# A gated-recurrence and feed-forward kernel on TensorE: k's transposes, masks, loads and the order of attention's passes from the ninth chunk on

## The chip, the cores and the metric

The kernel runs on one core of a Trainium2 chip. A core has TensorE (PE, matrix products; its weight loads are listed as PEld), VectorE (DVE), ScalarE (ACT), GpSimd (POOL) and SyncE (SP), which here only issues transfers. The metric is the device time of one execution in microseconds (us); lower is better. The profile's span of the execution is some 2 us shorter than that time.

## The reference

A gated linear recurrence over 768 tokens, for 4 sequences of 8 heads of size 48, and then a feed-forward block with SiLU on the 3072 resulting rows. Cut to what is computed:

```python
# q, k, v, alpha: (4, 8, 768, 48) float32; alpha in 0.8 .. 1.0
state = np.zeros((B, H, D, D))
for t in range(S):
    state = alpha[:, :, t, :, None] * state + np.einsum('bhd,bhe->bhde', k[:, :, t], v[:, :, t])
    y[:, :, t] = np.einsum('bhd,bhde->bhe', q[:, :, t], state)
x = y.transpose(0, 2, 1, 3).reshape(B * S, H * D)       # (3072, 384)
h = x @ w_in                                            # w_in (384, 2048)
out = (h * (1 / (1 + np.exp(-h)))) @ w_out              # w_out (2048, 384)
```

## The kernel before

The kernel cuts the tokens into 24 chunks of 128 (6 of each of the 4 sequences, taken in turn: chunk `n` is part `ci = n // 4` of sequence `b = n % 4`). Inside a chunk the recurrence is a masked attention: k is multiplied by a running product of alpha (`kp`), q by a running quotient (`qp`), `kp` and `qp` give the scores, the scores are masked to earlier tokens, and the masked scores times v are the values. What earlier chunks left in the state `st` is added with another product, and at the end of a chunk the state takes up the chunk's k and v, except in the last chunk of each sequence.

The feed-forward block is cut into pieces of about 2.6 us of TensorE each (`enter`: x times w_in, in a form with fewer products than the plain one; `leave`: g times w_out, likewise). A function `fill` sets pieces between attention's stages, so that TensorE has work while other engines prepare the next stage. The framework then orders the instructions of each engine; an instruction goes freely within its dependences unless `keep_in_program_order` pins it behind the one traced before it on its engine. Each engine takes its own instructions strictly in that order.

From chunk 9 on (`n >= NA`, `NA = 8` counted from 0) q, k and alpha are loaded so that VectorE's transposes alone turn them, and the products are laid out in halves of 64 tokens, of which one quarter of a score block is not needed and never computed.

The stages that the change touches (`...` marks cuts):

```python
    def products(n):                          # alpha, k -> kp ; then q -> qp in quotient()
        ...
        dve.tensor_tensor_scan(u[:, end - 1 :: -1], sg[:, end:0:-1], one[:, end:0:-1], 0.0, ALU.mult, ALU.add)
        dve.tensor_single_scalar(least[:, n, :], u[:, 0:end:W], 2.0**-64, ALU.max)
        kp = c["kp"] = turns(kps, n)          # one buffer from chunk 9 on
        ...
    def quotient(n, sg=None, q=None):
        ...
        p = turns(qps, n)                     # one buffer from chunk 9 on
        dve.tensor_tensor_scan(p[:, 0:end], sg[:, 0:end], iv[:, 0:end], 0.0, ALU.mult, ALU.add)
        ...
    def blank(n):                             # clears two PSUM banks for the scores
        if n < NA:
            return
        ps = ctxs[n]["blank"] = [ps_attn() for _ in range(2)]
        for t in ps:
            act.activation(t.rearrange("p j c -> p (j c)"), ident[:, 0:1].to_broadcast([128, 4 * C]),
                           AF.Copy, scale=0.0)

    def scores(n):
        c = ctxs[n]
        ci, b = c["ci"], c["b"]
        ps = c.pop("blank") if n >= NA else [ps_attn() for _ in range(2)]
        for j in (0, 2, 1, 3):
            for e in range(2 if n >= NA else 1):
                for u in range(2):
                    ...
                    pe.matmul(ps[u][at, j, t], lhsT=c["kp"][r, j, at], rhs=c["qp"][r, j, t],
                              start=True, stop=True)
        g = c["g"] = work.tile([128, 2, NP, C], F32, name="g")
        for u in range(2):
            if n < NA:
                act.copy(g[:, u], ps[u])
                gps.affine_select(g[:, u], g[:, u], ...)
                continue
            m = mask[:, :, None, :]
            dve.tensor_tensor(g[:, u].rearrange("p (o j) c -> p o j c", o=2),
                              ps[u].rearrange("p (o j) c -> p o j c", o=2),
                              m.to_broadcast([128, 2, NP // 2, C]), ALU.mult)
        if ci < NCH - 1:
            ps_k = ps_attn()
            for j in range(NP):               # NP = 4
                pe.transpose(ps_k[:, j, :], c["kp"][:, j, :], ident)
            c["kn"] = work.tile([128, NP, C], F32, name="kn")
            act.copy(c["kn"], ps_k)
        if ci > 0:
            s = st[b].rearrange("p j u e -> p j (u e)")
            for j in range(NP):
                act.mul(s[:, j], s[:, j], least[:, n, j : j + 1])

    def values(n):
        ...
        for i, (at, w, x) in enumerate(todo): # 16 products of v with g, 12 of the state with qp
            t, at = divmod(at, 4)
            pe.matmul(py[32 * at : 32 * at + 32, t, :], lhsT=w, rhs=x, ...)
        ...
        act.copy(xts[half][:, :, e * C : (e + 1) * C], py[:, 0:NKT])

    def states(n):
        ...
        if ci < NCH - 1:
            ps = ps_attn()
            for j in range(NP):
                for i in range(4):
                    r = slice(32 * i, 32 * i + 32)
                    pe.matmul(ps[r, j, 0:D], lhsT=c["kn"][:, j, r], rhs=vn[:, 2 * j + i // 2, 0:D],
                              start=True, stop=True)
            for u in range(2):
                ...
                if ci > 0:
                    dve.tensor_tensor(s, x, s, ALU.add)
```

The loop, and where the pieces of the feed-forward block come in:

```python
    for step in range(STEPS):
        ...
        stages = [[(scores, 1)], [(products, 0)], [(values, 1)], [(states, 1)]]
        ...
        elif step >= NA:
            stages = [[(scores, 1)], [(products, 0)], [(values, 1), (states, 1)], [(quotient, 0), (blank, 0)]]
        for slot, group in enumerate(stages):
            for stage, lag in group:
                n = step - lag
                ...
                stage(n)
                ...
                if stage is quotient and n + 1 < NT:
                    load(n + 1)
            fill(step, slot)
```

The results of `leave` are stored from tiles of 128x192 by SyncE (`nc.sync.dma_start(out[...], o)`), 48 stores in all.

## Time and profile before

Three runs took 561.36, 561.52 and 562.27 us, the median is 561.52. The profiled execution has a span of 559.1 us with 12435 instructions.

| engine | busy, us | share of the span | instructions |
|---|---|---|---|
| PE (matrix products) | 543.4 | 97% | 5074 |
| PEld (weight loads, beside PE) | 492.6 | 88% | 5074 |
| DVE (VectorE) | 448.1 | 80% | 821 |
| ACT (ScalarE) | 208.9 | 37% | 414 |
| POOL (GpSimd) | 20.8 | 4% | 44 |

The costliest groups on PE are those of the feed-forward block: 768 and 576 records of 128x192 for `leave` (133.6 and 100.0 us busy), 384 of 128x256 for the plain first pieces (88.3 us) and 640 of 128x256 for `enter` (161.4 us in four groups). Attention's groups are smaller: values 44.7 us, scores 38.2 us, states 12.3 us, transposes of k for the state 13.1 us. A float32 product shows as two records in the trace.

How to read it: a row of a group gives busy time and mean length of one instruction. Products overlap, so busy time divided by the count is less than the mean length. The chain of work that ended last is followed back from the last instruction, at each step to what released it. A line such as L982 is a line of the kernel: L759 the scores, L776 k's transposes, L802 the values, L817 the states, L860 the plain first pieces, L884 `enter`, L982 `leave`.

### The profile page before, as it was taken

How to read it: one execution, taken by the hardware profiler on the slowest of the kernel's cores; microseconds unless marked ns; L12 is line 12 of the kernel's file. 1: busy time of each engine (PE TensorE's matmuls, PEld its weight loads, DVE VectorE, ACT ScalarE, POOL GpSimd, SP SyncE). 2: the span in 40 equal slices, each digit the busy share in tenths (PEclk: the TensorE clock that was granted, in tenths of full speed). 3: DMA queues.
4: the chain of work that ended last, by engine and by line, in shares of the span. 5: the costliest groups of instructions: out<-in, count | busy, mean ns of one | idle time of the engine just before them, and what ended most of it. 6: DMA issues, size and time to landing. Idle time of an engine off the chain costs nothing.

```text
span 559.1 us, 12435 instructions
## 1 busy us (share of the span) xinstructions
PE 543.4 (97%) x5074; PEld 492.6 (88%) x5074; DVE 448.1 (80%) x821; ACT 208.9 (37%) x414; POOL 20.8 (4%) x44
## 2 busy tenths in 40 slices
PE   5999999999999999999999999999999999999996
PEld 3788887898999999899989999999898999999995
DVE  5887789956998799986998897899895885857731
ACT  3456653323233342442433442443443342332100
POOL 5110000300000000000000000000000000000000
PEclk9899999999999999999999999999999999999999
DMA  9999871143443333333425444435422123334200
GB/s 208 223 288 201 235 187 42 26 118 100 101 107 97 82 86 88 98 87 86 130 69 162 141 113 133 131 81 154 132 69 88 53 84 118 101 98 122 72 30 26
DMA packets 94417, 63.81 MB, mean 114 GB/s; under 512 B 55312, under 2 KB 86032, under 8 KB 94352
## 3 DMA queue, kind: packets, MB, share of 16 engines
q1 hardware_dynamic: 94352, 62.94, 43.2%
q8 instruction: 41, 0.67, 0.5%
q14 instruction: 24, 0.20, 0.1%
HBM read 58.20 MB, written 4.72 MB: 113 GB/s over the span
## 4 chain that ended last, share of the span: by engine, by line
PE 79%; DVE 12%; DMA 3%; ACT 2%; SPq 1%; issue 1%; POOL 0%; DVEq 0%; ACTq 0%
PE ps_o L982 35%; PE ps_m L884 21%; PE ps_m L860 11%; PE ps_a L802 6%; PE ps_a L759 3%; PE ps_a L776 2%; DMA qn<-in_q_dram 1%; DVE g L898 1%; DMA bits<-in_moe_w_in_dram 1%; DVE u L701 1%; PE ps_a L817 1%; DVE p L730 1%; DVE seen L665 1%; SPq L456 1%; DVE w_out L626 1%
## 5 line engine op out<-in xcount | busy, mean ns | idle before, releaser
L982 PE MATMUL ps_o<-w_out,g 128*128 128x192 f32 x768 | 133.6, 328 | 0.0
L982 PEld LDWEIGHTS ps_o<-w_out,g 128*128 128x128 f32 x768 | 125.5, 190 | 2.7 <-issue 0.6
L982 PE MATMUL ps_o<-wt,g 128*128 128x192 f32 x576 | 100.0, 327 | 0.0
L982 PEld LDWEIGHTS ps_o<-wt,g 128*128 128x128 f32 x576 | 95.1, 190 | 1.5
L860 PE MATMUL ps_m<-xt,w_in 128*128 128x256 f32 x384 | 88.3, 382 | 0.8 <-ACT xt L807 0.8
L860 PEld LDWEIGHTS ps_m<-xt,w_in 128*128 128x128 f32 x384 | 71.1, 190 | 10.6 <-ACT xt L807 1.2
L884 PE MATMUL ps_m<-xc,w_in 128*128 128x256 f32 x288 | 70.1, 379 | 0.0
L884 PEld LDWEIGHTS ps_m<-xc,w_in 128*128 128x128 f32 x288 | 54.0, 190 | 6.4 <-DVE g L898 0.2
L665 DVE TENSOR_REDUCE seen<-bits 128x1 f32<-128x384 int32 (+2 forms) x65 | 42.4, 689 | 15.1 <-DMA bits<-in_moe_w_out_dram 14.9
L895 ACT ACTIVATE g<-g 128x1024 f32<-128x1024 f32 x32 | 33.1, 1055 | 56.5 <-DVE g L898 56.5
L987 DVE TENSOR_TENSOR g<-g 128x512 f32<-128x512 f32 x72 | 48.4, 685 | 6.0 <-PE ps_o L982 5.9
L890 ACT COPY g<-ps_m 128x512 f32<-128x512 f32 x64 | 36.7, 586 | 36.1 <-PE ps_m L884 36.0
L884 PE MATMUL ps_m<-xc,wx 128*128 128x256 f32 x192 | 50.1, 383 | 0.0
L782 ACT ACTIVATE st<-st,least 128x96 f32<-128x96 f32 x80 | 24.1, 364 | 57.3 <-DVE least L704 57.3
L884 PEld LDWEIGHTS ps_m<-xc,wx 128*128 128x128 f32 x192 | 35.0, 190 | 4.2 <-issue 0.4
L898 DVE TENSOR_TENSOR g<-ps_m,g 128x512 f32<-128x512 f32 x56 | 37.3, 681 | 0.7 <-PE ps_m L884 0.5
L701 DVE TENSOR_TENSOR_SCAN u<-al,one 128x516 f32<-128x516 f32 x24 | 29.1, 1211 | 8.7 <-POOL mask L535 4.5
L730 DVE TENSOR_TENSOR_SCAN p<-al,inv 128x516 f32<-128x516 f32 x24 | 29.4, 1225 | 5.2 <-PE ps_a L802 4.9
L863 ACT ACTIVATE g<-ps_m 128x512 f32<-128x512 f32 x32 | 19.0, 594 | 38.7 <-PE ps_m L860 38.6
L802 PE MATMUL ps_a<-g,vn 128*32 128x128 f32 x768 | 27.9, 281 | 1.8 <-POOL g L766 1.7
L802 PEld LDWEIGHTS ps_a<-g,vn 128*32 128x32 f32 x768 | 20.4, 111 | 9.1 <-issue 5.6
L890 ACT COPY part<-ps_m 128x512 f32<-128x512 f32 x32 | 18.6, 582 | 21.8 <-PE ps_m L884 17.6
(125 smaller groups left out, 632.1 us busy)
## 6 DMA issues: line engine op xcount, KB each, us to landing
bits<-in_moe_w_in_dram SPq DMA_DIRECT2D x24, 512.0 KB, 4.8
bits<-in_moe_w_out_dram SPq DMA_DIRECT2D x32, 384.0 KB, 3.3
at<-in_alpha_dram SPq DMA_DIRECT2D x64, 96.0 KB, 2.3
kt<-in_k_dram SPq DMA_DIRECT2D x64, 96.0 KB, 2.4
qt<-in_q_dram SPq DMA_DIRECT2D x64, 96.0 KB, 2.5
bits<-in_alpha_dram SPq DMA_DIRECT2D x9, 512.0 KB, 3.4
out_dram<-o SPq DMA_DIRECT2D x48, 96.0 KB, 1.7
an<-in_alpha_dram SPq DMA_DIRECT2D x8, 192.0 KB, 5.2
```

Source lines behind the costliest of these rows:

```text
L665: dve.tensor_reduce(seen[kind][which][:, i : i + 1], x, axis=AX, op=op, apply_absolute_value=True))
L701: dve.tensor_tensor_scan(u[:, end - 1 :: -1], sg[:, end:0:-1], one[:, end:0:-1], 0.0, ALU.mult, ALU.add)
L730: dve.tensor_tensor_scan(p[:, 0:end], sg[:, 0:end], iv[:, 0:end], 0.0, ALU.mult, ALU.add)
L782: act.mul(s[:, j], s[:, j], least[:, n, j : j + 1])
L802: pe.matmul(py[32 * at : 32 * at + 32, t, :], lhsT=w, rhs=x, start=(i < 4), stop=(i >= len(todo) - 4), skip_group_check=True)
L860: pe.matmul(ps[:, e, :], lhsT=w_in[:, t, (f + e) * 128 : (f + e + 1) * 128], rhs=xt[:, t, :], start=(t == 0), stop=(t == NKT - 1))
L884: pe.matmul(ps[:, e], lhsT=block_w(w)[:, 2 * pair + e], rhs=block_x(grp, x), start=(first and e == 0), stop=(e == 1), skip_group_check=True)
L890: act.copy(to, ps)
L895: act.activation(x, x, AF.Silu)
L898: dve.tensor_tensor(to, a, b, op)
L982: pe.matmul(ps, lhsT=x, rhs=w[:, i], start=(first and i == 0), stop=(i == HF - 1), skip_group_check=True)
L987: dve.tensor_tensor(cells(grp, h, pair, *to), cells(grp, h, pair, *x), cells(grp, h, pair, *y), ALU.subtract)
```

## The change

From chunk 9 on:

- k for the state is no longer transposed by PE. `flip` lets VectorE transpose `kp` in blocks of 32x32 and stores the tile to DRAM; `land`, one step later, loads it back with four transfers that put the blocks in place. Its PSUM bank and ScalarE's copy go too.
- Masks: no clearing of PSUM before the scores and no product with a mask on VectorE. ScalarE copies the computed parts of the scores to SBUF (two copies of 128x256 elements, four of 64x128), and GpSimd masks the diagonal blocks in place with four selects of 64x256. The part that is never computed is zeroed once.
- Order: attention's products are pinned in program order (`in_order`), also ScalarE's scaling of the state and the sums for `enter`. The stages of a step are set anew: state and values last in the step, with `flip` behind them. The pieces come one slot later (`+ 3` for `+ 2`) and are left to the scheduler.
- Loads of alpha, k and q for the next chunk are issued one by one, each right behind the transpose that frees its tile, not all together at the end. The scaled q has a second buffer.
- 40 of the 48 output stores are issued by GpSimd instead of SyncE, and the output tile has three buffers for two.

The diff, cut to its core (`...` marks cuts; context left out):

```diff
+    def in_order(ins):
+        return tc.keep_in_program_order(ins) if late else ins
...
-    opool = pool("opool", 2)
+    opool = pool("opool", 3)
+    dram = pool("dram", 2, bass.MemoryType.DRAM)
...
-    mask = consts.tile([128, 2, C], F32, name="mask")
-    ...
+    decayed = fix.tile([128, 2 * NP * C], F32, name="g")
+    low, high = slice(0, CH), slice(CH, C)
+    earlier, later = [(low, 0), (high, 1)], [(low, 1), (high, 0)]
...
                 if name == "a":
                     turned(c[name], tokens(sg))
+                    load(n + 1, "a")
...
             turned(c["k"], ps["k"])
+            load(n + 1, "k")
...
-        p = turns(qps, n)
+        p = turns(qps if n < NA else [qps[0], late["p"]], n)
...
             turned(c["q"], q)
+            load(n + 1, "q")
...
-    def blank(n):
-        ...
+    def flip(n):
+        c = ctxs[n]
+        if n < NA or c["ci"] == NCH - 1:
             return
-        ...
+        t = late["turn"].tile([128, NP, C], F32, name="turn").rearrange("p c (j d) -> p c j d", j=NP)
+        dve.transpose(t, c["kp"].rearrange("p j (c i) -> p c j i", i=32))
+        c["flip"] = dram.tile([128, NP * C], F32, name="flips")
+        nc.sync.dma_start(c["flip"], t.rearrange("p c j d -> p (c j d)"))
+
+    def land(n):
+        c = ctxs[n]
+        if "flip" in c:
+            c["kn"] = work.tile([128, NP, C], F32, name="kn")
+            x = c.pop("flip").rearrange("(r d) (i x) -> i d r x", r=4, i=4)
+            for i in range(4):
+                nc.sync.dma_start(c["kn"][32 * i : 32 * i + 32], x[i])
...
-        ps = c.pop("blank") if n >= NA else [ps_attn() for _ in range(2)]
+        ps = [ps_attn() for _ in range(2)]
...
-                    pe.matmul(ps[u][at, j, t], lhsT=c["kp"][r, j, at], rhs=c["qp"][r, j, t],
-                              start=True, stop=True)
+                    in_order(pe.matmul(ps[u][at, j, t], lhsT=c["kp"][r, j, at],
+                                       rhs=c["qp"][r, j, t], start=True, stop=True))
...
-            m = mask[:, :, None, :]
-            dve.tensor_tensor(g[:, u].rearrange("p (o j) c -> p o j c", o=2), ...)
-        if ci < NCH - 1:
+        if n >= NA:
+            ps = [x.rearrange("p (o j) c -> p o j c", o=2) for x in ps]
+            for u in range(2):
+                act.copy(swapped[:, :, u, :, CH:], ps[u][:, :, :, CH:])
+            for r, o in earlier:
+                for u in range(2):
+                    act.copy(swapped[r, o, u, :, 0:CH], ps[u][r, o, :, 0:CH])
+            for at, half in ((CH, later), (0, earlier)):
+                for r, o in half:
+                    x = swapped[r, o].rearrange("p u j c -> p (u j) c")[:, :, at : at + CH]
+                    gps.affine_select(x, x, pattern=[[0, NP], [1, CH]],
+                                      compare_op=ALU.is_ge, fill=0.0, base=0, channel_multiplier=-1)
+        if n < NA and ci < NCH - 1:
             ps_k = ps_attn()
...
-                act.mul(s[:, j], s[:, j], least[:, n, j : j + 1])
+                mul = act.mul(s[:, j], s[:, j], least[:, n, j : j + 1])
+                if late:
+                    tc.keep_in_program_order(mul)
...
-            pe.matmul(py[32 * at : 32 * at + 32, t, :], lhsT=w, rhs=x, start=(i < 4), ...)
+            in_order(pe.matmul(py[32 * at : 32 * at + 32, t, :], lhsT=w, rhs=x, start=(i < 4), ...))
...
-                    pe.matmul(ps[r, j, 0:D], lhsT=c["kn"][:, j, r], ...)
+                    kn = c["kn"][:, j, r] if n < NA else c["kn"][:, i, 32 * j : 32 * j + 32]
+                    in_order(pe.matmul(ps[r, j, 0:D], lhsT=kn, ...))
...
-            combine(block_x(grp, to), sa, block_x(grp, a), sb, block_x(grp, b))
+            tc.keep_in_program_order(
+                combine(block_x(grp, to), sa, block_x(grp, a), sb, block_x(grp, b)))
...
-            nc.sync.dma_start(out[r : r + C, c * HO : (c + 1) * HO], o)
+            (gps if grp < NG - 1 else nc.sync).dma_start(out[r : r + C, c * HO : (c + 1) * HO], o)
...
-    marks = [2 * SLOTS + 2] + [(GB * i + 2 * GB) * SLOTS + 2 for i in range(len(phases))]
+    marks = [2 * SLOTS + 2] + [(GB * i + 2 * GB) * SLOTS + 3 for i in range(len(phases))]
...
-            stages = [[(scores, 1)], [(products, 0)], [(values, 1), (states, 1)], [(quotient, 0), (blank, 0)]]
+            stages = [[(land, 1), (scores, 1)], [(products, 0)], [(quotient, 0)],
+                      [(values, 1), (states, 1), (flip, 0)]]
...
-                if stage is quotient and n + 1 < NT:
-                    load(n + 1)
...
+            if step * SLOTS + slot == (NA + 1) * SLOTS - 1:
+                x = decayed.rearrange("p (o i c) -> p o i c", o=2, c=C)
+                for r, o in later:
+                    gps.memset(x[r, o, :, 0:CH], 0.0)
```

## The prediction

> **What bounds the kernel now.** I read the page's first two parts and its chain first, then the busy time by stretches, then the chain in order of time around the passes that change.
>
> The page: busy time and share of each engine, PE's row of the span in 40 slices, and the chain by engine.
>
> ```profile
> PE 543.4 (97%) x5074; PEld 492.6 (88%) x5074; DVE 448.1 (80%) x821; ACT 208.9 (37%) x414; POOL 20.8 (4%) x44
> ...
> PE   5999999999999999999999999999999999999996
> ...
> PE 79%; DVE 12%; DMA 3%; ACT 2%; SPq 1%; issue 1%; POOL 0%; DVEq 0%; ACTq 0%
> ```
>
> TensorE (PE) is busy 97% of the span and every slice but the first and last reads 9; the chain is 79% PE. VectorE (DVE), at 80%, is second and must be watched. The stretches (us, then busy us of PE, weight loads, DVE, ACT, POOL) say where PE's missing time lies:
>
> ```profile
> 0.00:60.00 60.00, 51.55 (x513) 41.99 (x514) 46.77 (x82) 29.61 (x58) 12.62 (x33) 0.97 1.06 230
> 60.00:300.00 240.00, 238.10 (x2564) 214.47 (x2563) 206.05 (x382) 95.06 (x202) 8.16 (x11) 1.00 0.39 103
> 300.00:460.00 160.00, 159.99 (x1469) 146.70 (x1468) 139.87 (x247) 62.98 (x121) 0.00 (x0) 1.00 0.39 108
> 460.00:550.00 90.00, 90.00 (x511) 86.00 (x510) 54.33 (x109) 21.28 (x35) 0.00 (x0) 1.00 0.28 86
> 550.00:559.00 9.00, 3.76 (x24) 3.46 (x22) 1.07 (x3) 0.00 (x0) 0.00 (x0) 0.89 0.11 33
> ```
>
> PE idles 15.6 us in all. 8.45 of it (60 less 51.55) fall before 60 us, 5.2 in the last 9 us (last product, addition, store), and only 1.9 us between 60 and 460 (all of it before 300), where attention and feed-forward pieces are interleaved. So no wait of weight can be removed there: PE is full, and what counts is PE work. In the stretch 300 to 460, DVE is busy 139.87 of 160 us, 87%, with little room.
>
> What one changed pass costs, from the chain in order of time (start, length, what). The first three lines are a chunk whose k is transposed on PE, the last three one of the final four chunks, which has no such transposes (they feed the state, and the last chunk of a sequence has no successor):
>
> ```profile
> 349.98 0.82 PE ps_a L759 x24
> 351.40 2.60 PE ps_o L982 x16
> 354.00 2.59 PE ps_m L884 x12
> ...
> 392.20 0.82 PE ps_a L759 x24
> 393.01 2.81 PE ps_o L982 x16
> 395.83 2.59 PE ps_m L884 x12
> ```
>
> From the start of the scores to the end of the piece behind them: 354.00 - 349.98 = 4.02 us with the four transposes, 395.83 - 392.20 = 3.63 us without. The transposes fill 0.6 us, but without them the next piece takes 2.81 instead of 2.60 us: the switch from the small score tiles to full 128x128 products costs 0.2 us, and the transposes had hidden it. One chunk's transposes are worth 0.39 us, not 0.6.
>
> **What the Trainium skill says.** "TensorEngine Tiling (Array Packing)", Key Properties: changing the tiling mode drains TensorE. The trace agrees: the 0.2 us above, and 2.79 or 2.80 us for most pieces behind the values and states. "VectorE: DVE Perf Modes", The three transpose paths: VectorE transposes only 32x32 blocks, TensorE a full 128x128; that is why the new path adds a trip through DRAM to arrange the blocks. "SBUF — State Buffer", Who interferes with whom: VectorE with two SBUF inputs and GpSimd reading SBUF exclude each other for an instruction. The trace before agrees in part: two GpSimd selects took 1.22 us at 117.07 us, with VectorE idle after 0.7 us, and 1.91 us at 12.49 us, where a VectorE scan ran beside them. "DMA: Bandwidth & Descriptors", SWDGE vs HWDGE vs iDMA: a transfer queued on GpSimd has its descriptors written by GpSimd's software. No transfer of the kernel before was queued there, so no row prices it.
>
> **The change part by part** (chunks 9 to 24; 12 of them pass a state on).
>
> The costs of rows that go:
>
> ```profile
> L770 DVE TENSOR_TENSOR g<-ps_a,mask 128x512 f32<-128x512 f32 x32 | 20.5, 683 | 3.5 <-PE ps_a L759 3.3
> ...
> L743 ACT ACTIVATE ps_a<-ident 128x512 f32<-128x512 f32 x32 | 19.0, 599 | 0.4
> ...
> L776 PE MATMUL ps_a<-ident,kp 128*128 128x128 f32 x80 | 13.1, 286 | 0.4 <-DVE st L823 0.4
> ...
> L778 ACT COPY kn<-ps_a 128x512 f32<-128x512 f32 x20 | 11.8, 588 | 8.4 <-PE ps_a L776 8.4
> ```
>
> 1. PE loses 12 x 4 = 48 of the 80 transposes: 12 x 0.39 = 4.7 us, all on the bound.
> 2. DVE loses the mask products, 32 x 683 ns = 21.9 us, and gains 12 block transposes. The same form for q takes 1109 ns, so + 13.3 us. Net -8.6 us (-0.26 us a chunk, -1.4 for the last four). Not on the path; it buys slack.
> 3. ACT loses 32 clearings x 599 ns = 19.2 us and 12 copies of the transposed k x 588 ns = 7.1 us. It gains, per chunk, two copies of 256 elements and four of 128. Copies of 192, 384 and 512 elements take 315, 474 and 589 ns, so about 370 and 262 ns: 2 x 0.37 + 4 x 0.26 = 1.8 us, x 16 = 28.6. Net + 2.3 us on an engine busy 37%. Hidden.
> 4. GpSimd gains 64 selects of 256 elements. 512 elements take 628 to 635 ns alone and 128 take 288, so about 0.4 us, 1.6 us a chunk; also 40 of the 48 stores' issues. It had 20.8 us of work. Hidden unless it comes late. VectorE may lose some 0.5 to 1 us a chunk of its new slack to the shared port.
> 5. DMA gains, 12 times, one store of 256 KB and four loads of 64 KB each. Loads of 96 KB land 2.3 to 2.5 us after issue and each holds SyncE about 0.45 us, so k is back some 7 us after its flip (2 for the store, 2 for issuing four, 2.5 to land). In the built order of PE's instructions, a chunk's state products come just before the next chunk's scores, about one round, 20 us, after its own scores. So the trip is hidden with over 10 us to spare. DMA is a third busy; 5 MB more is nothing.
> 6. The pinned order. In the built order values stand alone and states directly before scores: two visits to attention a round, as before, where values and states were together. So the number of exits stays (0.2 us each); entering the scores from the states may cost a little more, and one visit is split in two. I put 0.5 us for the whole. Between scores and values lie in most chunks some 6 products of 0.43 us per weight pair and a product of 2.6 us with its neighbours, 6 to 7 us; the new chain of copies and selects needs 1.8 + 1.6 = 3.4 us plus hand-overs. Hidden in most chunks, tight in the one with the split visit, where about 4.3 us remain.
> 7. A second buffer for the scaled q and loads issued as each tile comes free: before, the scan that makes it waited for the values' products (4.9 us in five waits). That lets DVE run ahead. Since PE idles only 1.9 us in this region, at most that comes back; I count 0.5.
>
> Sum: 561.5 - 4.7 + 0.5 - 0.5 = 556.8. For collisions in new places (four engines now work on one mask, ACT's burst of six copies and four state scalings holds up the emptying of the pieces' banks for up to 3 us) I add 0.5: 557.3 us, -0.8%.
>
> **The rivals.**
> A. GpSimd becomes the late one. Its queue runs in order and holds stores before selects; a store waits for its tile. SyncE waited 73.0 us in 33 waits, up to 5.6, for such tiles before. If a select stands behind one, the values are late and PE, whose order is now fixed, stands. 1 us a chunk is 16 us: 573 or more. Against it: the built order places values late enough for 3 us of delay, and the stores before a chunk's selects are mostly those of products finished earlier.
> B. DVE becomes the bound. At 87% with port conflicts it could fall behind by 0.5 us a chunk: + 8 us, 561 to 565. Against it: it loses more work than it gains, and the new slack of item 7.
> C. The trip through DRAM takes over as the wait, if SyncE's queue holds it behind loads that wait for their tiles. The loads behind it would slip too. Each us beyond the 10 spare costs 12 us: 565 or more. The measured landings speak against it.
> D. The gain is larger: both switches are absorbed or the 1.9 us idle vanish and the opening runs tighter. 551 to 553. More isn't there: 2% is 11.2 us, more than twice what the transposes hold.
>
> **Range and chances.** 557.3 us, with 552.5 to 565 for 8 in 10: below stands D, above the mild forms of A and B. Under 550.3 needs PE work that I can't find in the change, 0.05. Over 572.8 needs a stall of over 1 us in every chunk, 0.09. Within 2%: 0.86.
>
> **What would show it.** Right: PE's transposes of k fall from 80 to 32, PE busy falls by 4 to 6 us, the piece behind the scores reads 2.8 us, PE's idle time between 60 and 460 stays near 2 us, DVE's busy time falls by 5 to 9 us. Wrong: waits of the values' weight loads for GpSimd's mask (A), scores waiting for VectorE's q or k (B), state products waiting for the transfer of k (C), or PE idle between 60 and 460 above 6 us from anything. A drop of PE's busy time well beyond 5 us would mean that I mis-sized the switches.

## The result, and the profile after

The changed kernel takes 571.59 us (median of 4 runs, 569.73 to 572.67), the kernel before 561.89 us beside it: a ratio of 1.017, 95% interval 1.014 to 1.0199. It is 9.7 us slower, where 4.2 us faster was predicted, and lies above the 565 us at which the predicted range ended.

Three views of the profile after: the page's busy times and TensorE's row in 40 slices; groups of instructions by form (busy us, mean ns); and the stretches (us, then busy us of PE, weight loads, DVE, ACT, POOL, then PE's clock). The page's chain of waits ends after one VectorE addition here and says nothing, so the stretches and the order of time must carry the reading.

```profile
PE 546.7 (96%) x5026; PEld 489.2 (86%) x5026; DVE 445.9 (78%) x801; ACT 209.8 (37%) x466; POOL 78.7 (14%) x146
...
PE   5999999999999989999979999999999999999996
```

```profile
L806 POOL TENSOR_SCALAR_AFFINE_SELECT g<-g 64x256 f32<-64x256 f32 x64 | 36.8, 576 | 113.0 <-ACT g L799 91.8 <-ACT g L802 18.0
L1038 POOL DMA_DIRECT2D out_dram<-o x40 | 22.1, 552 | 244.3 <-DVE o L1035 157.3 <-ACT o L1033 79.8 <-ACT g L802 6.7
```

```profile
0.00:60.00 60.00, 52.77 (x512) 42.58 (x513) 46.22 (x82) 30.07 (x60) 11.15 (x29) 0.94 0.99 230
60.00:300.00 240.00, 232.00 (x2413) 205.15 (x2412) 202.11 (x367) 89.29 (x218) 40.52 (x65) 0.99 0.43 115
300.00:460.00 160.00, 157.84 (x1522) 143.04 (x1521) 135.20 (x231) 65.55 (x149) 22.67 (x44) 1.00 0.47 126
460.00:550.00 90.00, 88.42 (x490) 83.00 (x489) 56.73 (x114) 23.97 (x39) 4.34 (x8) 1.00 0.28 90
550.00:571.00 21.00, 15.70 (x97) 15.40 (x95) 5.61 (x11) 0.96 (x3) 0.00 (x0) 0.94 0.07 21
```

TensorE has its 48 instructions less (5026 for 5074) and is still busy 3.3 us longer. Between 60 and 460 us it stands for 8.0 + 2.2 = 10.2 us, where it stood for 1.9; the slices that read 8 and 7 are there. The transposes fell to 32, but the time that they held came back as standing time and more.

To see how much, I took the start of each TensorE product to the start of the next and subtracted what the same kind takes undisturbed (0.216 us a product of 256 columns, 0.1625 of 192, 0.123 a transpose as one of a run of four). Gaps over 0.25 us I call waits, smaller ones small losses; how large the sum of small losses is depends on what counts as a pass's own time, and only differences between kernels are used below. The sum of undisturbed times falls by 5.9 us, the 48 transposes. Past 60 us the small losses are 15.8 us instead of 11.0, the waits 15.2 instead of 2.9. Of the waits, 6.6 us are for VectorE's sums of x (`xc`), and what stands among them in its order, 3.5 us for GpSimd's masks, 2.4 us for additions of the output.

The longest waits, in order of time on TensorE (start, length, what, and in brackets the idle time and what ended it), kernel after:

```profile
278.10 1.08 PE L839 MATMUL ps_a<-g,vn 128*32 128x128 f32 x32
279.00 0.84 PE L839 MATMUL ps_a<-p,st 128*32 128x128 f32 x24
...
285.82 0.55 PE L855 MATMUL ps_a<-vn,kn 128*32 128x48 f32 x32
286.30 0.90 PE L786 MATMUL ps_a<-p,kp 48*64 48x128 f32 x32
287.42 1.99 PE L923 MATMUL ps_m<-xc,w_in 128*128 128x256 f32 x8 [0.23 <-DVE xc L575]
...
292.69 1.10 PE L923 MATMUL ps_m<-xc,w_in 128*128 128x256 f32 x4 [1.43 <-DVE xc L577]
295.04 2.59 PE L923 MATMUL ps_m<-xc,wx 128*128 128x256 f32 x6 [1.26 <-DVE xc L579]
```

The values (L839) are at 278.1, but the states (L855) only at 285.8, directly before the next scores. And VectorE begins the sums that the next pieces need only at 286.96, 8.9 us behind the values, kernel after:

```profile
282.17 0.43 DVE L732 TENSOR_TENSOR kp<-turn,u 128x256 f32<-128x256 f32 x1
...
284.64 0.68 DVE L751 TENSOR_TENSOR p<-turn,p 128x512 f32<-128x512 f32 x1
...
286.35 0.71 DVE L761 STREAM_TRANSPOSE turn<-kp 128x512 f32<-128x512 f32 x1
286.96 0.74 DVE L575 TENSOR_TENSOR xc<-xt 128x256 f32<-128x256 f32 x2
287.60 0.71 DVE L861 TENSOR_TENSOR st<-ps_a,st 48x192 f32<-48x192 f32 x2
```

VectorE isn't idle here: it does other work first, because that is its order. The sums (L575) stand directly behind the block transpose of the next chunk's k (L761), since `flip` is what is traced last on VectorE before the pieces; the state additions (L861) come after the first of them. So it is in the group before (block transpose at 202.81, first sum at 203.44); in the group after, where no chunk makes a block transpose any more, the first sum (380.59) stands directly behind the state additions (380.21). This is what the experiments had to explain. In the text "k's trip" is the block transpose on VectorE (`flip`), the store to DRAM and the loads back (`land`).

### The profile page after: what moved, and what is told of

Read it like the earlier page. It is cut to its first block, busy times and chain, and to the rows that moved or that the text cites. A ratio compares the mean times of both kernels' runs of the same rounds, so it can differ in the third digit from the quotient of the medians.

```text
span 570.3 us, 12645 instructions
## 1 busy us (share of the span) xinstructions
PE 546.7 (96%) x5026; PEld 489.2 (86%) x5026; DVE 445.9 (78%) x801; ACT 209.8 (37%) x466; POOL 78.7 (14%) x146
## 5 line engine op out<-in xcount | busy, mean ns | idle before, releaser
L1021 PE MATMUL ps_o<-w_out,g 128*128 128x192 f32 x768 | 135.6, 329 | 1.8 <-DVE o L1035 1.6
L923 PE MATMUL ps_m<-xc,w_in 128*128 128x256 f32 x288 | 71.3, 383 | 3.2 <-DVE xc L575 1.5
L923 PEld LDWEIGHTS ps_m<-xc,w_in 128*128 128x128 f32 x288 | 53.3, 190 | 11.3 <-DVE xc L575 2.1
L1038 POOL DMA_DIRECT2D out_dram<-o x40 | 22.1, 552 | 244.3 <-DVE o L1035 157.3
L923 PE MATMUL ps_m<-xc,wx 128*128 128x256 f32 x192 | 51.4, 393 | 2.6 <-DVE least L718 1.3
L806 POOL TENSOR_SCALAR_AFFINE_SELECT g<-g 64x256 f32<-64x256 f32 x64 | 36.8, 576 | 113.0 <-ACT g L799 91.8
L715 DVE TENSOR_TENSOR_SCAN u<-al,one 128x516 f32<-128x516 f32 x24 | 30.2, 1258 | 10.8 <-ACT al L712 10.5
L929 ACT COPY part<-ps_m 128x512 f32<-128x512 f32 x32 | 18.8, 588 | 43.6 <-PE ps_m L923 23.0
L839 PE MATMUL ps_a<-g,vn 128*32 128x128 f32 x768 | 28.3, 278 | 4.7 <-POOL g L806 2.9
L839 PEld LDWEIGHTS ps_a<-g,vn 128*32 128x32 f32 x768 | 20.2, 110 | 13.1 <-issue 6.6
```

The lines of the kernel that those rows point to most:

```text
L806: gps.affine_select(x, x, pattern=[[0, NP], [1, CH]], compare_op=ALU.is_ge, fill=0.0, base=0, channel_multiplier=-1)
L839: in_order(pe.matmul(py[32 * at : 32 * at + 32, t, :], lhsT=w, rhs=x, start=(i < 4), stop=(i >= len(todo) - 4), skip_group_check=True))
L923: pe.matmul(ps[:, e], lhsT=block_w(w)[:, 2 * pair + e], rhs=block_x(grp, x), start=(first and e == 0), stop=(e == 1), skip_group_check=True)
L929: act.copy(to, ps)
L1021: pe.matmul(ps, lhsT=x, rhs=w[:, i], start=(first and i == 0), stop=(i == HF - 1), skip_group_check=True)
L1038: (gps if grp < NG - 1 else nc.sync).dma_start(out[r : r + C, c * HO : (c + 1) * HO], o)
```

## The experiments

All times are medians; the ratio is to the kernel before, run beside it, with its 95% interval.

| run | us | ratio |
|---|---|---|
| changed kernel | 571.59 | 1.0170 [1.0140, 1.0199] |
| sums not pinned | 565.35 | 1.0051 [1.0035, 1.0067] |
| stores on SyncE | 586.29 | 1.0435 [1.0413, 1.0458] |
| masks as before | 575.04 | 1.0229 [1.0208, 1.0250] |
| before + k's trip | 589.84 | 1.0481 [1.0459, 1.0503] |
| before + k's trip + stores on GpSimd | 567.61 | 1.0103 [1.0086, 1.0120] |
| before + stores on GpSimd | 561.55 | 0.9992 [0.9985, 0.9999] |
| sums free, k by TensorE | 563.18 | 1.0024 [1.0012, 1.0037] |
| changed kernel, k by TensorE | 563.43 | 1.0027 [1.0013, 1.0041] |

**The pinned sums.** The changed kernel with one pin less:

```diff
-            tc.keep_in_program_order(
-                combine(block_x(grp, to), sa, block_x(grp, a), sb, block_x(grp, b)))
+            combine(block_x(grp, to), sa, block_x(grp, a), sb, block_x(grp, b))
```

> The changed kernel with one pin taken back: the sums for `enter` (11 small VectorE additions a group) may again be scheduled freely. Theory P (the pinned sums are the largest new wait): in the changed kernel TensorE stands about 6.6 us behind these sums at the head of three of the four groups (0.8 near 203 us, 3.4 from 287 to 294, 2.3 from 380 to 386); freed, they run as in the kernel before, some 3 us behind the copy of the last x, and the time falls by 4 to 7 us, to 565 to 567.5. Rival (the sums only show a VectorE that is late anyway through the masks and the shared port): the waits move to other instructions and the time stays within 1.5 us of 571.6.

565.35 us, 6.2 us less than the changed kernel. Behind the values at 274.2 the first sums now run at 278.6, and the piece that waited 1.43 and 1.26 us has waits of 0.44, 0.15 and 1.18 us. The first sum is 4.4 us behind the values instead of 8.9. So the pin costs 6.2 us here, but why it hurts was open: the sums are pinned behind something that is late.

**Stores and masks, each put back.** In the changed kernel all stores on SyncE again:

```diff
-            (gps if grp < NG - 1 else nc.sync).dma_start(out[...], o)
+            nc.sync.dma_start(out[...], o)
```

> The changed kernel with the 40 stores issued by SyncE again. The forecast's rival A in its first form (selects stand behind stores in GpSimd's queue): the values come earlier, the 3.5 us of waits for the mask near 188 and 209 us vanish and the time falls by 3 us or more. Against it: in the trace the four selects themselves take 2.3 to 4.2 us where they would take 1.6, without a store between; then this run is within 1.5 us of 571.6, and the stores are innocent.

586.29 us: 14.7 us more, which neither side of the expectation had. And the masks by ScalarE's clearing and VectorE's product again (`blank` and the mask tile come back, the copies and selects go; one `o` buffer less, for space):

```diff
-                act.copy(swapped[:, :, u, :, CH:], ps[u][:, :, :, CH:])      # ... 6 copies, 4 selects
+                dve.tensor_tensor(g[:, u]..., ps[u]..., m.to_broadcast(...), ALU.mult)
```

> The changed kernel with the masks of the kernel before: PSUM cleared by ScalarE, one product with a mask on VectorE for each half, no selects on GpSimd (the output tile has two buffers here, for space). Theory M (GpSimd's selects collide with VectorE and hold up both): the 3.5 us of waits for the mask vanish, VectorE's own operations beside the selects shorten, and the time falls by 4 us or more, to 567 or less. Rival (VectorE is close to its bound, and 1.4 us more a chunk puts it over): the time rises by 2 us or more. Theory P expects a fall of no more than the 3.5 us.

575.04 us, 3.5 us more. The new masks are a gain beside k's trip, although TensorE waits for them in two chunks. Those waits, first on TensorE and then on GpSimd, kernel after:

```profile
184.12 0.90 PE L786 MATMUL ps_a<-p,kp 48*64 48x128 f32 x32
184.95 2.86 PE L899 MATMUL ps_m<-xt,w_in 128*128 128x256 f32 x12
188.21 0.63 PE L839 MATMUL ps_a<-g,vn 128*32 128x128 f32 x12 [0.40 <-POOL g L806]
189.50 0.74 PE L839 MATMUL ps_a<-g,vn 128*32 128x128 f32 x18 [0.66 <-POOL g L806]
```

```profile
185.92 3.52 POOL L806 TENSOR_SCALAR_AFFINE_SELECT g<-g 64x256 f32<-64x256 f32 x4 [2.54 <-ACT g L799]
...
207.23 4.15 POOL L806 TENSOR_SCALAR_AFFINE_SELECT g<-g 64x256 f32<-64x256 f32 x4 [7.01 <-ACT g L802]
```

From the end of the scores to the values are 3.2 us here, and four selects take 3.52 us where 1.6 were counted. In 14 of the 16 chunks no wait for them is seen. The other way round, in the kernel with k by TensorE (see below), masks as before cost nothing:

> The version with free sums and k by TensorE (563.18 us), with the masks as before (ScalarE clears the banks, VectorE multiplies): 64 GpSimd selects and 96 short ScalarE copies go, 32 VectorE products of 683 ns come back. In the changed kernel that step cost 3.5 us. Theory V (masks off VectorE pay because VectorE carries the block transposes): without these it costs nothing, 562 to 563.5, or gains up to 1 us, since it drops the scores' longer way over three engines. Rival (masks off VectorE are worth 3 us for themselves): 565.5 to 567.

561.92 us, ratio 1.0002 [0.9993, 1.0012], 1.3 us less than with the new masks. The new masks gain with k's trip and the pinned sums and lose a little without both; which of the two makes the difference wasn't tried.

**k's trip alone.** The kernel before with `flip` and `land` and nothing else:

```diff
-            stages = [[(scores, 1)], ..., [(quotient, 0), (blank, 0)]]
+            stages = [[(land, 1), (scores, 1)], ..., [(quotient, 0), (blank, 0), (flip, 0)]]
```

> The kernel before with one part of the change alone: k for the state by VectorE's block transpose and a trip through DRAM, from chunk 9 on; masks, order, loads and stores as before. The forecast's first item alone: 12 x 0.39 = 4.7 us less, 557 us, if nothing else moves. In the built order the state products now stand alone, a third visit to attention in each chunk; by the 0.1 to 0.2 us that a switch costs in the trace that gives back 1.2 to 2.4 us, so 558.5 to 560. Rival (the trip is too slow and the state products wait for it): 565 or more, with waits for the transfer of k at the state products.

589.84 us, 28 us more than the kernel before, though no state product is seen waiting for the transfer of k. Its chain by engine, and SyncE's waits (us in total, times, longest):

```profile
PE 52%; DVE 23%; DMA 16%; issue 3%; ACT 3%; SPq 2%; POOL 0%; DVEq 0%; ACTq 0%
```

```profile
SPq L483 <- PE ps_a L839: 83.4, 13, 11.1
SPq L1020 <- DVE o L1018: 59.6, 18, 8.7
...
SPq L1020 <- ACT o L1016: 14.5, 5, 7.5
```

PE falls from 79% to 52% of the chain and DMA comes to 16% (10% are loads of weights, 2% loads of k as given; the transfers of the block-transposed k are not among the lines listed): the kernel now follows SyncE's queue. L1020 is the store of the output, L483 the reload of v. With the stores on GpSimd as well (the edit of the stores above, the other way round):

> The kernel before with k by VectorE and DRAM (alone 589.84 us) and with the stores issued by GpSimd as well. Theory H (SyncE's queue: a store that waits for its tile holds the block-transposed k and the weights behind it; the kernel before alone has nothing urgent behind them): most of the 28 us goes, 566 to 573 us. Rival D (VectorE is the cause: masks and block transposes both on it, 458 us busy): still 580 or more. Between lies a share of each; a third suspect is the reload of v, which waited 83 us for the states' products on the same queue and which stays.

567.61 us: 22.2 of the 28 us were stores that held up SyncE's queue, although the reload of v waited 95.8 us on the same queue. In the kernel before alone the same move of the stores is worth next to nothing:

> The kernel before with one part of the change alone: the stores of all groups of columns but the last are issued by GpSimd instead of SyncE. SyncE waited 103 us in the kernel before for the tiles of such stores. Theory H (that waiting was hidden there, since TensorE idled only 2.9 us past 60 us of the span; it became costly only once the trip of k through DRAM shared the queue): within 1 us of 562.3. Rival (a freed SyncE queue is worth something by itself, or the scheduler's order shifts): 2 us or more to either side; faster would make it the version that beats both.

561.55 us, ratio 0.9992. The waiting was hidden as long as the trip's 60 transfers were not on the same queue; whether their number or their urgency makes the difference isn't separated. It is also the only version that is below the kernel before, by 0.08%.

**k by TensorE again.** In the changed kernel, and in the one with free sums:

```diff
-        if n < NA and ci < NCH - 1:
+        if ci < NCH - 1:                       # 4 transposes and a copy per chunk again
-        ... flip, land ...                     # no block transpose, no store, no loads back
```

> The changed kernel (571.6 us), its sums still pinned, with k transposed by TensorE again. In the version with free sums that step took the time from a ratio of 1.0051 to 1.0024 to the kernel before. Theory of two separate causes: the pinned sums cost 6.2 us here too, 563.2 plus 6.2, about 569. Theory of one chain (the pinned sums are late only because VectorE's block transpose of k and what waits for it stand ahead of them in a VectorE that is full): without the block transposes the pin costs 2 us or less, 563 to 565, and TensorE's waits for the sums, 6.6 us in the changed kernel, fall below 2.

> The version with the sums free (565.35 us), with k transposed by TensorE again: 48 transposes of 128x128 and 12 ScalarE copies come back, the 12 VectorE block transposes and the 60 transfers through DRAM go. Theory T (the prediction's first item: a chunk's four transposes are worth 0.39 us because TensorE is full): plus 4.7 us, about 570. Rival U (what VectorE and SyncE lose to the trip costs about as much as TensorE gains: VectorE is late by 0.7 us and more a chunk, the weights by five transfers on SyncE's queue): within 1.5 us of 565.4, or below it; waits of TensorE for VectorE's masks and sums (about 9 us past 60 us of the span) would then shrink to 5 or less.

563.43 us with the sums pinned, 563.18 us with the sums free. Together with the first runs this is a table of two by two: with the trip 571.59 (pinned) and 565.35 (free), without it 563.43 and 563.18. The pin costs 6.2 us with the trip and nothing without; the trip costs 8.2 us with the pin and 2.2 without. In the changed kernel the pin is no cost by itself, and the trip a small one: its 2.2 us are 1.5 by the ratios, whose intervals just touch. That doesn't hold in every kernel: in the kernel before with the stores on GpSimd, where nothing is pinned, the trip costs 6.1 us (567.61 for 561.55). The stretches of the changed kernel with k by TensorE:

```profile
60.00:300.00 240.00, 237.88 (x2565) 215.22 (x2565) 206.90 (x373) 94.72 (x231) 37.62 (x66) 1.00 0.41 109
300.00:460.00 160.00, 160.00 (x1470) 146.75 (x1469) 130.68 (x227) 68.17 (x154) 22.41 (x44) 1.00 0.37 102
```

2.1 us of standing time instead of 10.2, with 48 transposes more. And the place in time that waited, same kernel:

```profile
275.28 1.08 PE L839 MATMUL ps_a<-g,vn 128*32 128x128 f32 x32
276.18 0.84 PE L839 MATMUL ps_a<-p,st 128*32 128x128 f32 x24
276.84 0.52 PE L855 MATMUL ps_a<-vn,kn 128*32 128x48 f32 x32
277.29 2.87 PE L1021 MATMUL ps_o<-w_out,g 128*128 128x192 f32 x16
280.09 0.90 PE L786 MATMUL ps_a<-p,kp 48*64 48x128 f32 x32
280.92 0.66 PE L811 MATMUL ps_a<-ident,kp 128*128 128x128 f32 x4
281.41 1.89 PE L923 MATMUL ps_m<-xc,w_in 128*128 128x256 f32 x8
```

VectorE, same kernel:

```profile
261.24 0.63 DVE L732 TENSOR_TENSOR kp<-turn,u 128x256 f32<-128x256 f32 x1
...
279.04 0.70 DVE L861 TENSOR_TENSOR st<-ps_a,st 48x192 f32<-48x192 f32 x2
279.77 1.10 DVE L575 TENSOR_TENSOR xc<-xt 128x256 f32<-128x256 f32 x3
```

The states start 1.6 us after the values, where it was 7.7 with the trip. The sums are pinned directly behind the state additions here and begin at 279.77, 4.5 us behind the values instead of 8.9, and no piece waits for them. And `kp` (L732) is written 18.8 us before its chunk's scores, where it was 4.1 with the trip; the mean of the 16 chunks is 15.6 us without the trip and 5.4 with it.

**Which half of the trip.** First the trip without VectorE's block transposes (what this leaves out: k comes back in the wrong arrangement, so the states are not the reference's):

```diff
-        dve.transpose(t, c["kp"].rearrange("p j (c i) -> p c j i", i=32))
-        nc.sync.dma_start(c["flip"], t.rearrange("p c j d -> p (c j d)"))
+        nc.sync.dma_start(c["flip"], c["kp"].rearrange("p j c -> p (j c)"))
```

> The changed kernel with the 12 block transposes left out: k goes to DRAM and back untransposed, so the states are built from k in the wrong arrangement; all else, the transfers and TensorE's products, is as in the changed kernel (571.6 us). Theory V (VectorE's 0.7 us a chunk, and the place it takes ahead of the sums, is what costs): 561 to 565, TensorE keeps its 5.9 us gain and the waits for sums go. Theory S (the trip's transfers and the states that depend on them cost): 568 to 571, with TensorE's waits for the sums still there.

Then the block transposes without the trip: k by TensorE for the states, `flip` keeps its `dve.transpose` and nothing reads it.

> The changed kernel with k transposed by TensorE for the states (563.4 us in that form), and VectorE's 12 block transposes made all the same, their result unused: no store to DRAM, no loads back. Theory V: 570 us or more, since the block transposes bring the waits back and TensorE's 48 transposes stay. Theory S: 563 to 566, as without the block transposes, plus at most what VectorE's 8.5 us of work cost by themselves.

572.63 us (ratio 1.0189 [1.0172, 1.0206]) and 563.50 us (1.0034 [1.0025, 1.0043]). VectorE's 8.5 us of block transposes cost nothing that can be told apart; what costs is the trip. In the first run the sums stand behind the state additions (285.11, first sum 285.84), late as in the changed kernel; in the second behind block transposes that come 22 us earlier (264.42 where it was 286.35). Yet hardly a product is seen waiting for a transfer: in the run without block transposes one wait of 0.76 us, in the changed kernel none. What the trip is seen to change is the order, on VectorE too: `kp` is ready 6.2 us before the scores in the first run and 15.5 in the second. That the transfers cost nothing by themselves is not shown: the trip made with its result unused, k by TensorE, wasn't run.

**The place of the states.** In the built order of the changed kernel each chunk's states stand directly before the next scores. The likely reason is that the scheduler expects k back only then; the reason itself wasn't tried, the place was. The states directly before the next scores without any trip (changed kernel, k by TensorE; the first steps of the loop, which differ, are left out here and below):

```diff
-            stages = [[(land, 1), (scores, 1)], [(products, 0)], [(quotient, 0)],
-                      [(values, 1), (states, 1), (flip, 0)]]
+            stages = [[(states, 2), (scores, 1)], [(products, 0)], [(quotient, 0)], [(values, 1)]]
```

> The changed kernel with k transposed by TensorE (563.4 us), and each chunk's state products moved from behind its values to directly before the next chunk's scores, where the trip had put them; no block transposes, no trip. Theory O (the place of the states is what costs: the state additions and the sums pinned behind them come late, the scores come late, the values stand alone): 570 to 577 us, with TensorE waiting over 3 us for the sums again. Theory X (the transfers on SyncE's queue cost): 563 to 565.

575.36 us (1.0226 [1.0210, 1.0241]), 11.9 us more than with the states behind the values. That is more than the trip costs, but the waits are of another kind; TensorE in that kernel:

```profile
161.30 0.55 PE L855 MATMUL ps_a<-vn,kn 128*32 128x48 f32 x32
161.77 0.90 PE L786 MATMUL ps_a<-p,kp 48*64 48x128 f32 x32
164.65 0.63 PE L811 MATMUL ps_a<-ident,kp 128*128 128x128 f32 x4 [1.98 <-DVE st L861]
```

States, scores and transposes follow each other without a piece between, and the transposes need a bank that VectorE's state addition has yet to empty: 9.0 us in all. Waits for sums, expected here, are not seen: in this version the sums are traced ahead of the states, and run ahead of them. So this isn't what happens in the changed kernel, which has no such transposes; and its order isn't reproduced either: the states are 4.5 us behind the values here, 7.4 to 16.7 there, and `kp` is ready 16.1 us before the scores, 5.4 there. The run shows that this place is dear with k's transposes on TensorE; that the place is what makes the trip costly is not shown.

The reverse: keep the trip, but put the states one chunk later behind the values, where k has long been back. In the version with free sums, and in the changed kernel itself:

```diff
+            stages = [[(scores, 1)], [(products, 0)], [(quotient, 0)],
+                      [(values, 1), (states, 2), (land, 1), (flip, 0)]]
```

> The version with free sums (565.35 us, ratio 1.0051), k by VectorE and DRAM as there, with each chunk's state products moved one chunk later, behind the next chunk's values (a state is next needed four chunks later), and the loads of k issued behind them. Theory O: the states are beside the values again and nothing waits for the trip: 558 to 561 us, ratio 0.993 to 0.998, below the kernel before, since TensorE keeps 48 transposes less (0.39 us a chunk, 4.7 us in the prediction) and the waits go. Theory X: 564 to 567, as the transfers are all still there.

> The same move of the states by one chunk, made in the changed kernel itself, its sums still pinned. Theory O: the pinned sums cost 2 us or less, since the state additions ahead of them are early: 559 to 563 us. If the pin costs by itself it stays 5 us or more above the version with free sums.

574.04 us (1.0199 [1.0185, 1.0213]) and 581.29 us (1.0327 [1.0306, 1.0349]), slower by 9 and 10 us: the expectation failed. TensorE in the first of them:

```profile
328.24 1.46 PE L922 MATMUL ps_m<-xc,w_in 128*128 128x256 f32 x6
330.79 0.90 PE L786 MATMUL ps_a<-p,kp 48*64 48x128 f32 x32 [1.09 <-DVE p L751]
```

Scores wait for the scaled q, 7.1 us in eight waits. On SyncE's queue the store of the block-transposed k now stood behind the loads of v and of the k before: issued at 314.8 us for a transpose of 308.8. Its tile is the one in which k and q are turned too. With `flip` traced directly behind the scaled q, ahead of those loads:

```diff
-            ..., [(quotient, 0)], [(values, 1), (states, 2), (land, 1), (flip, 0)]]
+            ..., [(quotient, 0), (flip, 0)], [(values, 1), (states, 2), (land, 1)]]
```

> The states one chunk later, as in the run before (574.0 us), with the block transpose and its store to DRAM traced directly behind the scaled q, ahead of the values and the loads of v and k. Theory O with the held tile: TensorE's waits for the scaled q go and 558 to 564 us remain, at or below the version with free sums (565.35). Theory R (one tile for three block transposes, of which one is held until its store has left, costs wherever the states stand; the trip only moves its wait): 566 to 574 us, with waits for q or k left.

567.35 us (1.0098 [1.0072, 1.0124]): the waits for q are gone and 6.7 us with them, as the held tile says, but it is still 2.0 us above the version with free sums (2.6 by the ratios). Its waits are 7.4 us, its small losses 19.8 us instead of 14.0. I have no cause for those; what an order with the trip and without its losses would take stays open.

**Parts that don't matter.** In the version with free sums (565.35), no pins at all, and the three loads of a chunk issued together again:

```diff
-        return tc.keep_in_program_order(ins) if late else ins
+        return ins
```

```diff
-                    load(n + 1, "a")           # and "k", "q", each as its tile comes free
+                    load(n + 1)                # all three, behind the quotient
```

> The version with the sums free, and now attention's products and the state scalings free too: no pin is left. Theory P, widened (any pin only holds work back on full engines): a little faster, 562 to 565 us. Rival Q (the pins keep the scheduler from placing values and states where their operands are not yet there; that is why they were set): slower by 3 us or more, 568 and above, with more visits to attention a chunk. The prediction's sixth item, 0.5 us for the pinned order, would leave it within 1 us of 565.4.

> The version with the sums free, with the three loads of the next chunk (a, k, q: four transfers each) issued together behind the scaled q, as the kernel before does, instead of each as its tile comes free. Theory L (loads as tiles come free keep VectorE ahead; they were given 0.5 us in the prediction): within 1 us of 565.4. Rival: issued together they hold SyncE for 12 times 0.45 us ahead of the block-transposed k and the weights, and VectorE's scans start late: plus 3 us or more, with VectorE's idle time before the turning of a, k and q grown by over 5 us.

564.45 us (1.0039 [1.0027, 1.0052]) and 564.34 us (1.0044 [1.0026, 1.0061]). Both intervals overlap that of the version they start from. Last, with k by TensorE and free sums (563.18), the pieces released one slot earlier, as in the kernel before (`SLOTS + 2` for `SLOTS + 3`):

> The version with free sums and k by TensorE (563.18 us, ratio 1.0024), with the feed-forward pieces released one slot earlier, as in the kernel before. Its TensorE has hardly a wait left but some 3 us between 478 and 537 us, behind the last chunk, where feed-forward pieces follow each other closely. Theory W (released a slot later, more pieces are left for that end, where each waits for the one before): 561 to 562, at or a little below the kernel before. Rival: the mark moves nothing there, since all pieces are released by then: 563.2, within 0.6.

564.05 us (1.0051 [1.0034, 1.0067] for 1.0024 [1.0012, 1.0037]), if anything slower. The waits at the end are gone, as expected, but three for the addition of an output, of 1.42, 1.42 and 0.90 us, stand at 230, 317 and 403 us in their place.

## Why the prediction was wrong

**Item 6, the pinned order: the step that failed.** I saw in the built order that states now come directly before the scores, counted the visits to attention, found two as before, and put 0.5 us for the whole, with another 0.5 us for collisions. Counting exits was the wrong measure. The runs showed in its place that the pin on the sums costs 6.2 us as long as k's trip is there (571.59 to 565.35) and nothing without it (563.43 and 563.18): with the trip, what the sums are pinned behind, the block transpose or the state additions, comes late, and the first sum stands 8.9 us behind the values instead of 4.5. Why the order around the trip is later stays open: the place of the states, the shorter lead of `kp` and the transfers on SyncE's queue come together with it, and no run separates them. Against the same kernel with k by TensorE, the sum of small losses is 5.3 us larger (15.8 for 10.5): 1.3 us of it are the switches between kinds of product, and 4.0 us lie in runs of feed-forward products and inside the passes. Of these 4.0, some 1.7 us belong to this execution: from 295 to 299 us products of 256 columns started 0.43 us apart instead of 0.216, and the clock granted from 290 to 300 us was 0.83. Some 1.3 us more are second products behind a switch, which start 0.10 us late (40 of them for 27). The waits are 9.4 us larger (15.2 for 5.8). That is 14.7 us in place of 1.0, or 13.5 if what item 1 had already counted for the bare switch (5.9 less 4.7) is taken off. Set against 5.9 us less of work it makes 8.8; the last product ends 8.9 us later in the trace, and the times differ by 8.2.

**Item 1, the transposes.** 80 fell to 32, and 0.39 us a chunk was a fair price in the order of the kernel before. But it is a price inside that order. Here TensorE's work falls by 5.9 us, and busy time rose by 3.3 instead of falling by 4 to 6.

**Item 5, the trip.** No product waited for the transfer, as predicted, but the working was wrong. In seven chunks k was back 8.2 to 11.3 us after its block transpose, in the last five 18.9 to 23.0, where 7 were counted; before the states 9.2 to 13.8 us were to spare in the seven, but only 0.2 to 3.1 in the five, not over 10. There the loads back (L771) stood on SyncE's queue behind a load of `bits` (L668) that waited for its tile, kernel after:

```profile
268.60 0.33 SPq L479 DMA_DIRECT2D at<-in_alpha_dram  x1
279.19 0.33 SPq L668 DMA_DIRECT2D bits<-in_alpha_dram  x1
279.61 1.81 SPq L771 DMA_DIRECT2D kn<-flips  x4
```

That is what rival C feared, just short of a wait. Where the stores were left on that queue it cost far more (14.7 and 22.2 us); the change had taken care of that.

**Item 4, GpSimd.** Selects take 576 ns on average, 407 at the least and 2517 at the most, for 0.4 us estimated. "SBUF — State Buffer", Who interferes with whom, in the Trainium skill says that VectorE with two SBUF inputs and GpSimd reading SBUF exclude each other; the four selects of 4.15 us ran beside the sums and a scan on VectorE, which took 0.45 us instead of 0.42 and 1.26 instead of 1.21, so GpSimd paid nearly all of it there. At 289 us VectorE paid too: beside selects of 0.74 and 0.49 us a sum took 0.62 us instead of 0.42. One reading in the prediction is wrong: beside the two selects at 117.07 us VectorE was idle for the first 0.7 us and then ran a transpose, and 1.22 us is what two such selects take undisturbed (0.63 us each, the second starting 0.59 us after the first). "Tight in the one with the split visit" held: the waits are there, 3.5 us. Rival A in its first form, a select behind a late store, isn't seen.

**Items 2, 3 and 7.** VectorE fell by 2.2 us, not 8.6: the block transpose took 706 ns instead of the 1109 estimated, but other groups grew, such as the scans of u by 1.1 us and the sums by 0.6; the rest is spread thinly and I can't place it. It made no difference: 8.5 us of block transposes alone cost nothing (563.50 for 563.43), so rival B, more work than VectorE can do, isn't seen; what TensorE waits for is VectorE's order. ScalarE's copies took 375 and 265 ns for 370 and 262 estimated, and its sum rose by 0.9 us for 2.3. The loads are worth nothing that can be told apart.

The test that I had named, standing time between 60 and 460 us above 6 us, did its work: it read 10.2.

## What to carry to other kernels

On a full engine, what an instruction takes out is a gain only if the order around it stays; look in the built order at where the consumer of a slower path now stands, and at what stands behind that consumer on every engine, before counting switches. Parts of a change should be tried in pairs: here the pin was free without the detour, and the detour cost 2 us instead of 8 without the pin. And a queue whose waits are hidden today may not stay so: before more is put on it, take off what waits there.

## What was not expected of the hardware

- A GpSimd select of 64x256 elements takes 0.41 us undisturbed and up to 2.5 us beside VectorE work. The VectorE instructions beside the longest grew by up to 9% (0.46 us for 0.42), a sum beside shorter ones by 48% (0.62 for 0.42, at 289.5 us).
- VectorE's block transpose of 128x512 took 0.71 us for `kp` and 1.11 us for alpha, k and q as loaded, the same form by the profile. No run here says why.
- Switches of TensorE between kinds of product, as loss per switch in the kernel after (from the start of the last product to the start of the next kind's first, less the mean step within the pass): values to feed-forward 0.17 us, scores to feed-forward 0.14, states to scores 0.12, feed-forward to any of them 0.09; in the kernel before, values to states read 0.06. The second feed-forward product behind a switch starts another 0.10 us late. So states split off from the values cost some 0.3 us, an estimate: 0.17 + 0.10 + 0.09 - 0.06.
- A store issued by GpSimd took 0.55 us there in the kernel after, one issued by SyncE 0.33 to 0.43 us of that queue in the kernel before (median 0.36).
